# Loading q's weight matrix with five DMAs of 128 rows instead of one

## The chip, the cores and the metric

The kernel runs on one core of one Trainium2 chip. The time is the device time of one execution in microseconds; the median of the runs counts. A profile is one more execution, taken with the hardware profiler; its span runs from the first instruction to the last, and the execution's own time has some 1.8 us around it.

## The reference

A transformer block in the parallel form: one layer norm feeds an attention and a feed-forward network, and both results are added to the input. The attention is local and dilated: each position looks at 8 positions, 0, 2, ..., 14 steps back, with 32 heads of 20 numbers each. S is 2048, D is 640, F is 1536, all in bf16.

```
xn  = layernorm(x)                                     # (S, D)
q, k, v = split(xn @ wqkv)                             # wqkv: (640, 1920), 32 heads of 20
logits[h, s, w] = q[h, s] . k[h, s - 2 w] * 20**-0.5   # w = 0..7, masked where s - 2 w < 0
attn = softmax(logits, over w)
o[h, s] = sum_w attn[h, s, w] * v[h, s - 2 w]
out = x + o @ wo + gelu(xn @ w1 + b1) @ w2 + b2        # w1: (640, 1536), w2: (1536, 640)
```

## The kernel before

The 2048 positions are handled in four chunks of 512, each of four blocks of 128 rows. A block is normalised with its rows on the partitions (`xn`), then transposed so that the 640 features lie on the partitions in five slices of 128 (`xnT`). For chunk 0 the transposes are done by TensorE (`do_tp`, L280) and copied out of PSUM by VectorE or ScalarE (`do_tc`, L285); for the other chunks a DMA transposes. q, k and v of a chunk are 15 groups of matmuls over the five slices; attention products and sums are done by VectorE; the feed-forward network's first layer goes through L586 and both output projections are summed in PSUM by L622 and L624.

The order of all work on all engines is written out by hand: the table ORDER names every piece once, and each engine runs its instructions in that order. Nothing is rescheduled; a wait on an engine holds all that stands behind it there.

The change lies ahead of this table, in the loads that are issued at the kernel's start. Most are issued by SP, one after the other, and share 16 DMA engines with the two that ScalarE issues. In order, SP's are: block 0 of x (`load_x(0, 1)`, L130), q's weights, k's weights (`load_w`, L133), blocks 2 and 3 of x, v's weights, blocks 4 to 7, and w1 in two halves (L146). Blocks 8 to 15 follow where `ldx` stands in ORDER. ScalarE issues block 1 (L137) and the 12 rows of the bias b1 (L138). The weights of q, k and v are columns 0 to 639, 640 to 1279 and 1280 to 1919 of the matrix in memory; each lands in a tile of 128 partitions x 5 x 640 (`wq_sb`, `wk_sb`, `wv_sb`), where the second index, written t in the view `wqkv_v`, is the group of 128 rows, that is, the slice of `xnT` that it is multiplied with.

Each DMA counts up one of eight semaphores as it lands, and the DMAs of SP and ScalarE take these eight in turn; a DMA that takes a semaphore again waits for the earlier one on it.

On TensorE the start runs like this. Ones are multiplied until block 0 is there (`do_warm`, L446). Block 0 is transposed in two parts, slices 0 and 1 (`tp00a`) and slices 2 to 4 (`tp00b`); the bias is transposed (`tb`, L456). Then q of block 0 is computed slice by slice: for each slice ti five matmuls of 128 columns, one for each output tile (`q_piece`, L349; the pieces are `ga` for slices 0 and 1, `gb2`, `gb3`, `gb4`). The transpose of block 1 (`tp01`) stands between `gb2` and `gb3`; q of block 1 follows (`gd` and `ge`, 25 matmuls), then k of blocks 0 and 1 (`hj100` to `hj102`, L380, 25 matmuls of 256 columns), the transpose of block 2 (`tp02`), five matmuls of v, the transpose of block 3 (`tp03`), and so on. Statistics of blocks 0, 2 and 3 are taken by VectorE (L209, L211), the square root by ScalarE (L245), reciprocal and normalisation by VectorE (L251, L265).

The order around the change, from the table's first lines:

```
wa ho st00a sum1 st00 rs00 rc00 neg1 sq1 xn00a tp00a wb xn00b tp00b mean1 tc00a rs01 rc01 tb b1 tc00b ga gb2 xn01 tp01
tc01a tc01b gb3 gb4 gd ge gc4 gc1 hj100 st02a st02 rs02 hc100 st03a st03 hj101 gc0 rc02 xn02 rs03 hj102 rc03 xn03
hc101 hc102 tp02 tc02 hj202 tp03 tc03 hj201 ...
```

Of the kernel before, what the change touches and what calls it, by code (L numbers as in the profile page):

```python
# [16 lines left out]
S, D, F, H, W, DIL = 2048, 640, 1536, 32, 8, 2  # L17
# [3 lines left out]
KT, FT = D // P, F // P  # L21
# [54 lines left out]
def kernel(  # L76
# [16 lines left out]
    nc = tc.nc  # L93
# [24 lines left out]
    wqkv = [wts.tile([P, KT, D], BF16, name=f"w{s}_sb") for s in "qkv"]  # L118
# [6 lines left out]
    wqkv_v = A_wqkv.rearrange("(t p) n -> p t n", p=P)  # L125
# [6 lines left out]
    def load_w(s):  # L132
        nc.sync.dma_start(wqkv[s][:], wqkv_v[:, :, s * D : (s + 1) * D])  # L133
# [2 lines left out]
    nc.vector.memset(x_sb[:, 1, 0:16], 0.0)  # L136
    nc.scalar.dma_start(x_sb[:, 1, :], x_nb[:, 1, :])  # L137
    nc.scalar.dma_start(b1_rt[0:FT, :], B_b1.rearrange("(t p) -> t p", p=P))  # L138
    load_w(0)
    load_w(1)  # L140
    load_x(2, BPC)
    load_w(2)
# [645 lines left out]
```

## Time and profile before

| what | value |
|---|---|
| median of 3 runs | 207.1 us (206.86 to 207.37) |
| the profiled execution: time | 207.49 us |
| the profiled execution: span | 205.7 us |
| granted TensorE clock | 1.00 |
| busy: TensorE, VectorE, ScalarE, GpSimd | 98%, 85%, 62%, 17% of the span |
| q's weights: issue, KB, time to landing | 1.20 us, 800 KB, 5.5 us |
| read from HBM, written to it | 10.00 MB, 7.54 MB |

The loads of the start fill the 16 DMA engines until about 20 us; in this row of the profile each figure is the mean of one of 40 equal slices (5.14 us) of the span:

```profile
GB/s 210 390 397 370 75 232 326 403 102 185 64 116 264 99 186 181 142 192 124 207 198 113 144 107 64 0 16 182 41 0 132 162 193 162 192 41 17 30 52 64
```

Columns of a timeline line are the start in us, the duration, engine, line, operation and tiles, and in brackets the idle time before it and what ended that. PE is TensorE's matmul, PEld its weight load, DVE VectorE, ACT ScalarE, POOL GpSimd, SP SyncE; a q behind the name (SPq) is the engine's own instruction queue, from which it issues DMAs.

### The profile page before, as it was taken

The page shows a single profiled execution, that of the slowest core. Times are in us where ns is not written, and L with a number is a line of the kernel's source. Part 1 is how long each engine was busy: PE and PEld are TensorE (multiplying, and loading weights), DVE is VectorE, ACT ScalarE, POOL GpSimd, SP SyncE. Part 2 cuts the span into 40 slices and gives each one's busy share as a digit, 9 for nine tenths or more (in the row PEclk, how much of TensorE's full clock was granted, in tenths as well). Part 3 has the DMA queues.
Part 4 walks back from the last instruction along what each step waited for, and adds up shares of the span by engine and source line. Part 5 has one row for each costly group of instructions (what it writes and reads, how often), then busy time and mean ns, then how long its engine had stood idle before and what let it go on. Part 6 is the DMA issues. An engine that isn't in the chain of part 4 may idle for free.

```text
span 205.7 us, 3262 instructions
## 1 busy us (share of the span) xinstructions
PE 200.8 (98%) x1285; PEld 112.2 (55%) x1285; DVE 175.4 (85%) x214; ACT 127.7 (62%) x242; POOL 34.4 (17%) x49
## 2 busy tenths in 40 slices
PE   7899999999999999999999999999999999999994
PEld 2797745565445555555555554555444555555552
DVE  3489999379998989949999994999979979799981
ACT  5488999899999879916466344834616854221210
POOL 2000000050000422102703303001023420311210
DMA  6999389969258599899996965018209998931244
GB/s 210 390 397 370 75 232 326 403 102 185 64 116 264 99 186 181 142 192 124 207 198 113 144 107 64 0 16 182 41 0 132 162 193 162 192 41 17 30 52 64
DMA packets 27335, 31.77 MB, mean 154 GB/s; under 512 B 9272, under 2 KB 22072, under 8 KB 27320
## 3 DMA queue, kind: packets, MB, share of 16 engines
q0 software_dynamic: 7408, 12.78, 39.4%
q1 hardware_dynamic: 19600, 18.58, 31.4%
q8 instruction: 10, 0.16, 0.3%
q10 hardware_dynamic: 312, 0.20, 0.3%
q14 instruction: 5, 0.04, 0.1%
HBM read 10.00 MB, written 7.54 MB: 85 GB/s over the span
## 4 chain that ended last, share of the span: by engine, by line
PE 95%; DMA 3%; SPq 0%; DVE 0%; issue 0%
PE lo L622 29%; PE hps L586 25%; PE pps L336 24%; PE hi L624 7%; PE gps L380 7%; DMA wq_sb<-in_A_wqkv_dram 3%; PE L L474 2%; PE gps L349 1%; PE tp L280 0%; SPq L130 0%; DVE osb L652 0%
## 5 line engine op out<-in xcount | busy, mean ns | idle before, releaser
L586 PE MATMUL hps<-xnT,w_sb 128*128 128x512 bf16 x240 | 55.6, 379 | 0.0
L433 DVE TENSOR_TENSOR half<-qT,kT 128x2560 bf16<-128x2560 bf16 x32 | 46.2, 1482 | 2.9 <-PE L L474 2.8
L622 PE MATMUL lo<-w_sb,hT 128*128 128x512 bf16 x144 | 41.3, 379 | 0.0
L586 PEld LDWEIGHTS <-w_sb 128*128 128x128 bf16 x240 | 22.9, 98 | 26.3 <-issue 0.8
L629 ACT CAST osb<-lo 128x512 bf16<-128x512 f32 x15 | 8.8, 587 | 36.8 <-PE hi L624 18.5
L624 PE MATMUL hi<-w_sb,hT 128*128 128x128 bf16 x144 | 31.5, 219 | 0.0
L602 ACT ACTIVATE hT<-hps,b1T 128x512 bf16<-128x512 f32 x36 | 24.0, 683 | 10.7 <-PE hps L586 10.7
L465 DVE TENSOR_TENSOR half<-half 128x2048 bf16<-128x2048 bf16 (+1 forms) x32 | 29.0, 952 | 0.2
L635 POOL DMA_DIRECT2D out_dram<-osb x15 | 13.6, 973 | 77.1 <-ACT osb L630 68.5
L557 DVE TENSOR_TENSOR half<-vT,x_sb 128x2560 bf16<-128x2560 bf16 x16 | 22.8, 1485 | 4.4 <-DMA x_sb<-e 3.0
L557 DVE TENSOR_TENSOR half<-vT,ax 128x2560 bf16<-128x2560 bf16 x16 | 22.8, 1485 | 2.3 <-PE L L474 1.4
L622 PEld LDWEIGHTS <-hT 128*128 128x128 bf16 x144 | 14.1, 98 | 16.8
L622 PE MATMUL lo<-wo,oT 128*128 128x512 bf16 x80 | 23.1, 379 | 0.0
L567 POOL DMA_DIRECT2D half<-half x12 | 14.3, 1195 | 48.9 <-DVE half L557 48.5
L336 PE MATMUL pps<-xnT,wv_sb 128*128 128x512 bf16 x75 | 18.5, 379 | 0.0
L336 PE MATMUL pps<-xnT,wq_sb 128*128 128x512 bf16 x75 | 18.3, 379 | 0.0
L336 PE MATMUL pps<-xnT,wk_sb 128*128 128x512 bf16 x75 | 17.7, 379 | 0.0
L624 PE MATMUL hi<-wo,oT 128*128 128x128 bf16 x80 | 16.9, 219 | 0.0
L173 ACT ACT_TABLE_LOAD x12 | 15.4, 1283 | 0.9 <-PEq L772 0.7
L624 PEld LDWEIGHTS <-hT 128*128 128x128 bf16 x144 | 14.1, 98 | 2.2
L573 DVE TENSOR_TENSOR half<-half 128x1280 bf16<-128x1280 bf16 x16 | 13.1, 820 | 1.3 <-DMA half<-half 1.2
L622 PEld LDWEIGHTS <-oT 128*128 128x128 bf16 x80 | 7.8, 98 | 9.4
(91 smaller groups left out, 263.7 us busy)
## 6 DMA issues: line engine op xcount, KB each, us to landing
half<-half POOLq DMA_DIRECT2D x12, 640.0 KB, 7.1
w_sb<-in_B_w_dram SPq DMA_DIRECT2D x4, 960.0 KB, 11.0
out_dram<-osb POOLq DMA_DIRECT2D x15, 160.0 KB, 4.0
ax<-e SPq DMA_DIRECT2D x8, 256.0 KB, 4.8
x_sb<-e SPq DMA_DIRECT2D x8, 256.0 KB, 4.8
out_dram<-b2bc POOLq DMA_DIRECT2D x3, 640.0 KB, 8.7
x_sb<-in_A_x_dram SPq DMA_DIRECT2D x1, 1280.0 KB, 12.9
out_dram<-x_sb SPq DMA_DIRECT2D x2, 640.0 KB, 8.7
```

The source lines that it names most:

```text
L173: nc.scalar.activation(warm[:], nc.const_aps.tensor(0.0, [P, 1], F32), func)
L336: nc.tensor.matmul(ps[:], lhsT=wqkv_p[which][:, ti, to, :], rhs=xnT[:, ti, :], start=(ti == 0), stop=(ti == KT - 1),)
L380: nc.tensor.matmul(ps[:, to - a, :], lhsT=wqkv_p[which][:, ti, to, :], rhs=tiles["xnT", 0][:, ti, pair * 2 * P : (pair + 1) * 2 * P], star ...
L433: nc.vector.tensor_tensor(out=half[:, j, h], in0=q[:, :, at].unsqueeze(1).to_broadcast([P, W // 2, KT, P]), in1=window(k, h, at), op=ALU.mult,
L465: nc.vector.tensor_tensor(out=kept, in0=kept, in1=gone, op=ALU.add)
L557: nc.vector.tensor_tensor(out=half[:, j, h], in0=window(qkv_tile(n, 2), h, cs), in1=ax_view(n)[:, j, ws, :].unsqueeze(2).to_broadcast([P, ...
L567: nc.gpsimd.dma_start(a, b, accum_op=ALU.add, max_dma_last_dim=CUT)
L586: nc.tensor.matmul(ps[:], lhsT=w1_sb[:, ti, ft * P : (ft + 1) * P], rhs=tiles["xnT", n][:, ti, :], start=(ti == 0), stop=(ti == KT - 1),)
L602: nc.scalar.activation(hT, tiles["hps", n, ft][:], ACT.Gelu_apprx_tanh, bias=b1T[:, ft : ft + 1], scale=1.0)
L622: nc.tensor.matmul(lo[:], lhsT=lhs, rhs=rhs[:, 0:CH], start=first, stop=last)
L624: nc.tensor.matmul(hi[:, 0 : D - CH], lhsT=lhs, rhs=rhs[:, CH:D], start=first, stop=last)
L635: nc.gpsimd.dma_start(rows, tiles["osb", n, bl][:], accum_op=ALU.add)
```

## The change

The one DMA for q's weights is replaced by five, one for each group of 128 rows, into the same tile and from the same queue. Everything else, ORDER included, is as before. Each group of matmuls that uses a slice of the tile now waits for that slice's DMA. Four more of the eight semaphores are taken, so that a later load waits for another one of its predecessors than before. Behind the change all lines of the file are two lines further down.

```diff
     nc.vector.memset(x_sb[:, 1, 0:16], 0.0)
     nc.scalar.dma_start(x_sb[:, 1, :], x_nb[:, 1, :])
     nc.scalar.dma_start(b1_rt[0:FT, :], B_b1.rearrange("(t p) -> t p", p=P))
-    load_w(0)
+    for a in range(5):
+        ks = slice(a * KT // 5, (a + 1) * KT // 5)
+        nc.sync.dma_start(wqkv[0][:, ks, :], wqkv_v[:, ks, 0:D])
     load_w(1)
     load_x(2, BPC)
     load_w(2)
```

## The prediction

> **What bounds the kernel now.** I read the page first (busy time), then the chain of work that ended last, in order of time, then the waits of TensorE, then the timeline of the first 20 us, and last the DMA issues and a table of one-microsecond stages.
>
> ```profile
> PE 200.8 (98%) x1285; PEld 112.2 (55%) x1285; DVE 175.4 (85%) x214; ACT 127.7 (62%) x242; POOL 34.4 (17%) x49
> ```
>
> TensorE is busy for 200.8 of 205.7 us. The chain says where the other time is, and the waits of TensorE (line and releaser: us in total, times, longest) say it again:
>
> ```profile
> 1.20 5.51 DMA wq_sb<-in_A_wqkv_dram
> 6.76 1.03 PE gps L349 x15
> ```
>
> ```profile
> PE tp L280 <- DVE xn L265: 0.8, 1, 0.8
> ...
> PE gps L349 <- DMA wq_sb<-in_A_wqkv_dram: 0.6, 1, 0.6
> ```
>
> The chain hangs on the load of q's weights until 6.71 (1.20 + 5.51), and from 6.76 on it is TensorE almost to the end. TensorE has no recorded wait after that, so a microsecond won or lost there goes through to the end unless a later hand-over is tighter than it. The part of its idle time that this load causes is 0.6 us. That is all the change can win at its place.
>
> The timeline (start, duration, engine, line, operation) shows what else could have gone on then, and what comes 6 us later:
>
> ```profile
> 1.20 0.42 SPq L133 DMA_DIRECT2D wq_sb<-in_A_wqkv_dram  x1
> 1.67 0.52 SPq L133 DMA_DIRECT2D wk_sb<-in_A_wqkv_dram  x1
> 2.23 0.53 SPq L130 DMA_DIRECT2D x_sb<-in_A_x_dram  x1
> ...
> 5.76 0.29 DVE L285 COPY xnT<-tp 128x256 bf16<-128x256 bf16 x1
> 6.00 0.18 PE L456 MATMUL tb<-ident,b_rt 16*128 16x16 bf16 x1
> ...
> 9.60 0.89 DVE L209 BATCH_NORM_STATS2 stats<-x_sb 128x6 f32<-128x320 bf16 x2 [1.20 <-DMA x_sb<-in_A_x_dram]
> ...
> 11.79 0.45 DVE L265 TENSOR_SCALAR xn<-x_sb,mv,rstd 128x640 bf16<-128x640 bf16 x1
> 12.48 0.38 PEld L280 LDWEIGHTS <-xn 128*128 128x128 bf16 x5
> ```
>
> The first two slices of xnT, which the first ten matmuls on q need, are there at 6.05 (5.76 + 0.29). VectorE sat idle before 9.60 until blocks 2 and 3 of x landed; the normalised block 2 that follows from them is ready at 12.24 (11.79 + 0.45), and TensorE takes it at 12.48. So this hand-over has 0.24 us to spare, and 0.06 of that is the usual step between the engines (an earlier one: xn ends at 5.66, TensorE starts at 5.72).
>
> ```profile
> wk_sb<-in_A_wqkv_dram SPq DMA_DIRECT2D x1, 800.0 KB, 7.1
> ...
> x_sb<-in_A_x_dram SPq DMA_DIRECT2D x1, 320.0 KB, 7.3
> ```
>
> ```profile
> 2.00:3.00 1.00, 1.00 (x4) 0.43 (x3) 0.00 (x0) 0.22 (x2) 0.00 (x0) 1.00 0.88 269
> 3.00:4.00 1.00, 1.00 (x5) 0.36 (x4) 0.72 (x2) 0.37 (x1) 0.00 (x0) 1.00 1.02 328
> 4.00:5.00 1.00, 0.65 (x6) 0.32 (x4) 0.54 (x3) 0.93 (x5) 0.00 (x0) 1.00 1.04 386
> ```
>
> The last column is SDMA GB/s, the one before it the share of the 16 engines: from 2 us on they are full (0.88, 1.02, 1.04), up to 20 us. The loads are one stream; each lands when the bytes ahead of it are through. wk lands at 1.67 + 7.1 = 8.8, blocks 2 and 3 at 2.23 + 7.3 = 9.5.
>
> **Part 1: the first matmuls on q start earlier.** They need the first piece instead of all five. Bytes through, by the stage rows: 0.04 MB before 2.0, then 0.269, 0.328 and 0.386 a microsecond, 1.02 MB by 5.0. Block 0, block 1 and all of q are 1120 KB = 1.15 MB, through at 5.3; q landed 1.4 us later, at 6.7. By the same count the pieces are through at 3.5, 4.0, 4.4, 4.8 and 5.3, and with the same 1.4 us land at about 4.9, 5.4, 5.8, 6.2 and 6.7. TensorE is done with tb at about 6.1 and wants the pieces at 6.1, 6.5, 6.8, 7.4 and 7.8 (five matmuls take 0.35 us: 1.03 / 15 x 5; five transposes stand between the third and the fourth). All are there. Gain at this place: 6.76 - 6.1 = 0.6 us, and 50 matmuls on q end near 9.4 instead of 10.0. Then wk is wanted at 9.2 (its weight load started at 9.80) and has landed at 8.8: no wait.
>
> **Part 2: what takes the gain back.** The 25 matmuls on wk (2.73 us) then end some 0.6 us earlier, and the next thing on TensorE is the transpose of block 2. It can't start before 12.24 + 0.06 = 12.30, since its chain hangs on the landing at 9.5, not on TensorE: statistics of both blocks, square root, reciprocal, L265. So TensorE arrives 0.6 early and waits 0.4: of the 0.6 us, 12.48 - 12.30 = 0.18 stays. Block 3's hand-over is like it (L265 ends at 13.10, TensorE takes it at 13.30). Behind them the half of w1 that landed at about 18.5 is taken at 19.03, with 0.4 to spare, more than 0.18. I found no later hand-over from VectorE that is tighter: the sums for the logits end at 36.13 and are taken at 36.53.
>
> **Part 3: what the four added DMAs cost.** SP issues one in 0.42 us, with 0.46 to 0.47 from issue to issue (0.74, 1.20, 1.67). wk's issue moves from 1.67 to 1.20 + 5 x 0.46 = 3.50, and all of SP's loads behind it move. Data begins to move at 1.8 (the DMA view of the first two microseconds), 1.06 us after the first issue, so wk could move from 4.56; its turn is at 5.3. That is 0.7 us of cover, by which the added issues cost nothing; the work that hides them is the stream itself, already queued. If an issue takes what the next two took (0.52, 0.53, so 0.57 from one to the next), wk can move from 5.1 and the cover is 0.2; by the small bias load on ScalarE's queue (0.64) it is 0.36 late. Bounds of this cost: 0 to 0.36; I take 0, since 0.42 is the row of the same tensor.
>
> Also, eight completion semaphores are used in turn, so from the ninth load on each waits for an earlier one. In the changed program wk waits for block 0 (landed at 0.74 + 2.5 = 3.2, before SP gets there), blocks 2 and 3 for q's first piece, wv for its second, blocks 4 to 7 for block 1, the halves of w1 for q's third piece and the bias, blocks 8 to 15 for q's fourth. Before, the first two of these waits stood at the halves of w1. Blocks 2 and 3 are then issued at about 4.9 and can move from 6.0; their turn is at 5.3 + 2.1 = 7.4. wv is issued at about 5.4, can move from 6.5, and its turn is at 8.2. Behind the waiting load stand all later loads of SP, and each has over a microsecond of cover. Cost 0; without cover, each microsecond late goes to TensorE but for the 0.18.
>
> The price of a border between two transfers in the stream has no row of its own. From above: block 0 alone, 160 KB, took 2.5 us to land, 2.1 more than its bytes at 390 GB/s. From below: blocks 2 and 3 land 0.7 us after wk, for 320 KB, which at 390 GB/s are 0.84; nothing is left for the border. I take 0, as the queue is full there just as it will be for q. A gain is possible too: in 1.8 to 3.8 us the stream ran at 174, 287, 315 and 329 GB/s in half-microsecond stages, 0.58 us behind a steady 390; pieces that read the matrix in another order may lose less or more there.
>
> **Sum.** -0.6 at q, +0.4 at block 2's transpose, 0 for issues, waits and borders: -0.2 us. The profiled execution took 207.5 (span 205.7 and 1.8 around it), 0.4 above the median of 207.1; so 207.3 for a like execution, and 206.9 for the median.
>
> **Rivals.**
> 1. The landing of blocks 2 and 3 comes earlier with the pieces. Place: the stream before 4 us. For it: the 0.58 us lost there. Against it: q's bytes and rows are the same. From 0.4 us earlier on, nothing takes the gain back: -0.6, so 206.5.
> 2. The stream falls behind (the other side). Place: SP's queue. Its price is the time by which a load is ready after its turn, and it decides from 0.2 us on, when block 2's transpose comes later than now. For it: wk's cover falls from 2.6 us (1.67 + 1.06 against 5.3) to 0.7, and a piece (0.42 us of data at 390 GB/s) takes 0.46 to issue. Against it: the cover above. If none of it holds, the whole shift of wk's issue shows, 1.8 us: blocks 2 and 3 at 11.3, TensorE 1.6 late, 208.7; with half, 207.8.
> 3. The change doesn't do what it says: the pieces land together, near 6.7, as completions come late on a full queue. For it: q landed 1.4 us after its bytes were through. Then 207.1.
> 4. Every transfer carries its lone overhead in series: four times 2.1 us. Blocks 2 and 3 at 17.9, TensorE 8.2 late, 215.3. Against it: the 0.7 us between wk and blocks 2 and 3.
>
> Beside rival 4 stands a rule of the Trainium skill, "DMA: Bandwidth & Descriptors", sections "Anatomy of one DMA" and "Rules for kernel authors": it fits about 2.0 us fixed per DMA on GpSimd's path, and asks for transfers of 1 MiB and more, small ones being joined. By that fit in series four more transfers would be an estimated 8 us. The trace doesn't agree where the queue is full, by the 0.7 us for 320 KB.
>
> **How the numbers follow.** Forecast 0.50, rival 1 0.17, rival 2 0.23, rival 3 0.07, rival 4 0.03. A measurement of this kernel tells about 0.3%, 0.62 us, from no change; the three runs shown lie 0.5 us apart. Faster by more: half and a little of rival 1 (its 0.6 sits at the bound), 0.10, and 0.02 of the forecast's scatter: 0.12. Slower by more: most of rival 2, 0.19, rival 4, 0.03, and 0.02 of scatter: 0.24. Within: 0.64. The range takes in rival 1 and the part of rival 2 up to some 0.8 us: 206.4 to 207.9, leaving out about 0.18. The likeliest case alone: 206.6 to 207.2.
>
> **What would show it.** Right: the first L349 at about 6.1, no DMA wait of q among TensorE's waits, in its place a wait of the transpose (L280) for L265 of about 0.4 us near 12; blocks 2 and 3 landing at 9.5; wk issued near 3.5. Part 1 is wrong if L349 still waits for a piece; part 3 is wrong if the stage rows before 8 us fall below 380 GB/s or blocks 2 and 3 land after 9.7. The forecast falls if that landing moves by more than 0.4 us either way, or if a later hand-over shows a new wait of TensorE.

## The result, and the profile after

The changed kernel takes 210.47 us (median of 6 runs, 209.93 to 212.05), the kernel before 207.26 us (6 runs, 206.86 to 207.44): slower by 3.2 us, a ratio of 1.0165 with a 95% interval of 1.0131 to 1.0198. The forecast was 206.9 us, its range 206.4 to 207.9. The profiled execution took 210.40 us, its span is 208.6 us, 2.9 more than before.

First the timeline of the changed kernel, for the same places as in the prediction (start, duration, engine, line, operation; in brackets the idle time before and what ended it). All lines are two further down, so L349 is L351, L280 is L282, L209 is L211 and L265 is L267:

```profile
1.21 2.31 SPq L141 DMA_DIRECT2D wq_sb<-in_A_wqkv_dram  x5
3.56 0.44 SPq L133 DMA_DIRECT2D wk_sb<-in_A_wqkv_dram  x1
4.05 0.52 SPq L130 DMA_DIRECT2D x_sb<-in_A_x_dram  x1
...
6.04 0.75 PE L351 MATMUL gps<-xnT,wq_sb 128*128 128x128 bf16 x10
...
11.65 0.89 DVE L211 BATCH_NORM_STATS2 stats<-x_sb 128x6 f32<-128x320 bf16 x2 [3.97 <-DMA x_sb<-in_A_x_dram]
...
13.84 0.45 DVE L267 TENSOR_SCALAR xn<-x_sb,mv,rstd 128x640 bf16<-128x640 bf16 x1
14.34 0.45 PE L282 MATMUL tp<-ident,xn 128*128 128x128 bf16 x5 [0.58 <-DVE xn L267]
```

The first matmuls on q start at 6.04 instead of 6.76, as forecast. But the statistics of blocks 2 and 3, which started at 9.60, now wait for their DMA until 11.65, and the transpose of block 2 starts at 14.34 instead of 12.48 (there its weight load, which the prediction shows; its matmul stood at 12.59): some 1.8 us late. The DMA view (KB, us from issue to landing) and the waits of TensorE say what else came late:

```profile
wq_sb<-in_A_wqkv_dram SPq DMA_DIRECT2D x5, 160.0 KB, 3.6
wk_sb<-in_A_wqkv_dram SPq DMA_DIRECT2D x1, 800.0 KB, 7.2
...
x_sb<-in_A_x_dram SPq DMA_DIRECT2D x1, 320.0 KB, 7.6
```

```profile
PE gps L382 <- DMA wk_sb<-in_A_wqkv_dram: 1.5, 1, 1.5
PE tp L282 <- DVE xn L267: 1.2, 2, 0.6
```

wk lands at 3.56 + 7.2 = 10.8 instead of 8.8, blocks 2 and 3 at 4.05 + 7.6 = 11.6 instead of 9.5. TensorE waits 1.5 us for wk and the rest in front of block 2. The issues are not at fault: wk's stands at 3.56 for a forecast of 3.50, blocks 2 and 3 are issued at 4.05 for about 4.9, and SP was held by no semaphore before either. The stream itself lost the time. Stage rows (last column GB/s, before it the share of the DMA engines):

```profile
3.00:4.00 1.00, 1.00 (x5) 0.32 (x4) 0.79 (x2) 0.42 (x1) 0.00 (x0) 1.00 0.99 340
4.00:5.00 1.00, 0.77 (x7) 0.36 (x5) 0.50 (x4) 0.94 (x5) 0.00 (x0) 1.00 0.72 133
5.00:6.00 1.00, 0.63 (x8) 0.47 (x8) 0.96 (x4) 0.97 (x3) 0.00 (x0) 1.00 0.93 324
...
8.00:9.00 1.00, 1.00 (x22) 1.00 (x20) 0.00 (x0) 0.20 (x1) 0.00 (x0) 1.00 1.01 311
```

From 4 to 5 us, where it had 386 GB/s, it has 133, and until 10 us it stays between 303 and 348 where it had 374 to 396. In the stall eight packets take 420 to 850 ns each, for 55 ns elsewhere.

The 16 DMA engines don't come through together, and a load has landed when the last of them has. Blocks 2 and 3 were through on eight engines by 8.56 before and by 9.55 after, on 15 by 8.92 and by 10.85, on the last by 9.58 and by 11.63, with the statistics starting at 9.60 and 11.65. So about 1.0 us of the 2.05 is common to the engines, and the rest lies in the slowest of them.

The shift of TensorE, matmul against matmul, stays at 1.76 to 1.83 us up to 180 us and is 2.06 at the last matmul (0.2 come at 183 us, where ScalarE waits for an output buffer until an output DMA has landed). The span is 2.9 us longer. So 0.8 us are lost behind the last matmul. The end of the kernel before and then of the changed one, in the timeline (a line of several matmuls ends at start plus duration):

```profile
core 0 of [0], span 205.7 us
...
202.51 0.44 PE L624 MATMUL hi<-wo,oT 128*128 128x128 bf16 x5
202.82 0.36 SPq L644 DMA_DIRECT2D out_dram<-osb  x1
...
203.31 0.37 ACTq L657 DMA_DIRECT2D out_dram<-osb  x1
```

```profile
core 0 of [0], span 208.6 us
...
204.57 0.44 PE L626 MATMUL hi<-wo,oT 128*128 128x128 bf16 x5
204.87 0.36 SPq L646 DMA_DIRECT2D out_dram<-osb  x1
...
205.37 0.37 ACTq L659 DMA_DIRECT2D out_dram<-osb  x1
```

From the last matmul's end to the end of the span it is 2.78 us before (202.95 to 205.73) and 3.60 after (205.01 to 208.61). The last two output DMAs are issued with the same distance to the matmul, and land with it: 1.61 and 1.8 us behind it in both. What follows them differs. SP waits for the eight DMA semaphores, 103 to 110, one after the other. The trace's records of these waits, by their start in us behind the last matmul's end:

```
before: last DMAs on 109 and 110. waits: 103 0.60, 104 0.67, 105 0.74, 106 0.80, 107 0.86, 108 0.92, 109 1.63, 110 1.88, drain 1.95
after:  last DMAs on 105 and 106. waits: 103 0.49, 104 0.55, 105 1.63, 106 1.89, 107 1.95, 108 2.01, 109 2.07, 110 2.16, drain 2.64
```

With four more DMAs the turn has moved on by four, so that the last two landings stand third and fourth in SP's list. Of the 0.82 us that the end is longer, 0.28 are the rest of the list (110 is through at 2.16 for 1.88), 0.41 are a longer step from there to the drain (0.48 for 0.07), and 0.13 come behind the start of the drain.

### The profile page after: what moved, and what is told of

Read it like the earlier page. It is cut to its first block, busy times and chain, and to the rows that moved or that the text cites. A ratio compares the mean times of both kernels' runs of the same rounds, so it can differ in the third digit from the quotient of the medians.

```text
span 208.6 us, 3244 instructions
## 1 busy us (share of the span) xinstructions
PE 200.3 (96%) x1263; PEld 112.2 (54%) x1285; DVE 175.4 (84%) x214; ACT 127.6 (61%) x242; POOL 34.4 (17%) x49
## 4 chain that ended last, share of the span: by engine, by line
PE 87%; DMA 6%; SPq 1%; DVE 1%; issue 1%; ACT 1%; ACTq 0%
PE lo L624 25%; PE hps L588 25%; PE pps L338 23%; PE hi L626 7%; PE gps L382 5%; DMA x_sb<-in_A_x_dram 4%; DMA out_dram<-osb 3%; PE L L476 2%; SPq L141 1%; DVE stats L211 1%; ACT osb L631 1%; PE tp L282 0%; DVE xn L267 0%; SPq L133 0%; DVE mv L213 0%
## 5 line engine op out<-in xcount | busy, mean ns | idle before, releaser
L588 PE MATMUL hps<-xnT,w_sb 128*128 128x512 bf16 x229 | 55.0, 379 | 0.6
L624 PE MATMUL lo<-w_sb,hT 128*128 128x512 bf16 x139 | 40.3, 379 | 0.1
## 6 DMA issues: line engine op xcount, KB each, us to landing
x_sb<-in_A_x_dram SPq DMA_DIRECT2D x1, 1280.0 KB, 12.4
```

Of the source, the lines that this page charges most:

```text
L588: nc.tensor.matmul(ps[:], lhsT=w1_sb[:, ti, ft * P : (ft + 1) * P], rhs=tiles["xnT", n][:, ti, :], start=(ti == 0), stop=(ti == KT - 1),)
L624: nc.tensor.matmul(lo[:], lhsT=lhs, rhs=rhs[:, 0:CH], start=first, stop=last)
```

## The experiments

The theories, in the order in which they came up. A: the loads have less lead over their turn. B: small DMAs are slow as such. C: the first reading of the matrix's later rows stalls, later put as C' (whoever reads unread rows piece by piece meets a slow start each time). D: small pieces at the start of the stream. L: a cut DMA stalls where its turn comes some 2 us after its issue; S, N and P are its rivals. R: the semaphore list at the end. M: the place of the tiles in memory. All times are medians; "before" is measured beside each group (207.2 to 207.3 us). Edits are against the kernel before, unless the changed one is named.

**Less lead alone.** q in one DMA; the loads behind it are held by a write into wk's tile until 3.52 us, close to where wk's issue stands in the changed kernel.

```diff
-    load_w(1)
 ...
+        nc.gpsimd.memset(wqkv[1][:, 0:3, :], 0.0)
+        load_w(1)
```

> q's weights are loaded by one DMA as before; only the issue of k's weights, and with it all SP loads behind it, is held back by a GpSimd fill of the tile until about 3.5 us (1.67 before, 3.56 in the changed kernel). Theory A (lead: the loads behind q are issued too late, so that engines come to the end of their queue and lose a microsecond each time): blocks 2 and 3 land at 11 to 12 us instead of 9.6, TensorE's transpose of block 2 some 2 us later, 209 to 210.5 us in all. Theory B (pieces: the borders of small transfers, or reading the matrix by row groups, slow the stream): they land at 9.6 to 9.8 and the time is 207.1 to 207.5.

207.46 us, ratio 1.0018 (1.0005 to 1.0031). The stage rows show one dip where wk's turn comes and then the full stream:

```profile
5.00:6.00 1.00, 0.53 (x7) 0.40 (x7) 0.94 (x5) 0.97 (x3) 0.00 (x0) 1.00 1.00 312
6.00:7.00 1.00, 1.00 (x18) 0.95 (x17) 0.73 (x4) 0.62 (x2) 0.00 (x0) 1.00 1.06 384
```

A falls as the whole cause: late issues of whole DMAs cost 0.2 us here by the median. (The profiled run, 208.67 us, is the slowest of the ten: there one DMA engine was late on blocks 4 to 7, which were through on 15 engines by 12.85 and on the last by 14.51. Blocks 2 and 3 landed at 9.16.)

**Small DMAs deep in the stream.** v by three DMAs.

```diff
-    load_w(2)
+    for ks in (slice(0, 2), slice(2, 4), slice(4, 5)):
+        nc.sync.dma_start(wqkv[2][:, ks, :], wqkv_v[:, ks, 2 * D : 3 * D])
```

> q by one DMA as before; v's weights, which are issued some 5 us before their turn, by three DMAs of 256, 256 and 128 rows. Theory A (lead): nothing is lost, blocks 4 to 7 land at 13.2 to 13.6 us, the stage rows from 8 to 11 us stay at 390 GB/s, 207.0 to 207.6 us. Theory B (pieces): the stage rows from 8 to 11 us fall below 360 GB/s and blocks 4 to 7 land 0.5 to 1.5 us later than 13.35.

207.68 us, ratio 1.0028 (1.0015 to 1.0042). In the stages of v's transfer nothing is lost:

```profile
8.00:9.00 1.00, 1.00 (x22) 1.00 (x20) 0.00 (x0) 0.20 (x1) 0.00 (x0) 1.00 1.07 393
9.00:10.00 1.00, 1.00 (x14) 1.00 (x12) 0.64 (x2) 0.65 (x2) 0.00 (x0) 1.00 1.08 396
```

B falls. (The 0.4 us belong to the end: 3.26 us behind the last matmul.)

**q in two DMAs, and q's five in another order.** In the changed kernel the loop becomes, in the one run, two DMAs of 2 and 3 row groups, and in the other five in the order 2, 0, 1, 3, 4.

```diff
-    for a in range(5):
-        ks = slice(a * KT // 5, (a + 1) * KT // 5)
+    for ks in (slice(0, 2), slice(2, 5)):
```

> q's weights by two DMAs, rows 0 to 255 and 256 to 639; one more issue on SP, so k's weights are issued at about 2.15 us instead of 1.67 or 3.56. Theory A (lead): most of the lead is kept, blocks 2 and 3 land at 9.5 to 10.0, the first matmul on q at 6.05, 206.9 to 207.5 us. Theory B (a loss for every border, 2.05 us over four): 0.5 us later per border, blocks 2 and 3 at 10.1, 207.4 us; the stall at 4 to 5 us is there in part.

> The five DMAs of the changed kernel in another order: rows 256 to 383 first, then 0, 128, 384, 512. Theory A (lead): the stall stands at the same time, 4 to 5 us, whichever rows are read there, and blocks 2 and 3 land at 11 to 12 us; 209.9 to 211 us. Theory C (the first read of rows from 256 on meets something slow in memory, which one DMA over all rows overlaps): the slow stretch moves to the first piece, about 3 us, and 4 to 5 us runs at over 300 GB/s.

208.76 us (1.0056 to 1.0105) and 209.64 us (1.0072 to 1.0149). The stage 4 to 5 us of the one and of the other:

```profile
4.00:5.00 1.00, 1.00 (x4) 0.29 (x3) 0.50 (x4) 0.97 (x5) 0.00 (x0) 1.00 0.77 233
```

```profile
4.00:5.00 1.00, 0.62 (x6) 0.32 (x4) 0.50 (x4) 0.95 (x5) 0.00 (x0) 1.00 0.71 161
```

One cut is enough, and the stall stays at its time whichever rows are read first: C falls as it was put. Both times lie above what I had expected under every theory. The trace of the one cut is of its slowest run (209.68 us); its blocks 2 and 3 landed at 11.4, nearly as late as behind four cuts (11.6).

**Rows read once before, and pieces of an unread matrix.** In the changed kernel a small DMA ahead of q's five reads a few bytes of every row, or of every sixteenth; in the kernel before, w1's first half is cut in five.

```diff
+    touch = consts.tile([P, KT, 8], BF16, name="touch")
+    nc.sync.dma_start(touch[:], wqkv_v[:, :, 0:8])
```

```diff
+    touch = consts.tile([8, KT, 8], BF16, name="touch")
+    nc.sync.dma_start(touch[:], A_wqkv.rearrange("(t p s) n -> p t s n", p=8, s=16)[:, :, 0, 0:8])
```

```diff
-        nc.sync.dma_start(w1_sb[:, :, cs], w1_v[:, :, cs])
+    for ks in [slice(a, a + 1) for a in range(5)]:
+        nc.sync.dma_start(w1_sb[:, ks, 0 : F // 2], w1_v[:, ks, 0 : F // 2])
+    nc.sync.dma_start(w1_sb[:, :, F // 2 :], w1_v[:, :, F // 2 :])
```

> The changed kernel with one DMA more: ahead of q's five pieces, a DMA reads 16 bytes of each of the 640 rows of the weight matrix into a spare tile that nothing reads. Theory C' (the pieces are slow because q is the first to read these rows, and one piece after another meets rows that nobody has read, which the single DMA meets all at once): with the rows read once before, the stall of the five pieces is gone; the stage 4 to 5 us is above 330 GB/s instead of 133, and x blocks 2-3 land, counted from their issue, within 6.3 us instead of 7.6; the small DMA itself costs up to some 1 us of the stream, so 207.3 to 208.7 us. Theory D (small pieces at the start of the stream are slow whatever was read before): a stage of under 240 GB/s stays between 4 and 6 us, x blocks 2-3 land at 11.5 us or later, 209.5 to 211.5 us.

> As the kernel with the small DMA over all rows, but the small DMA reads 16 bytes of every sixteenth row only (40 rows). C' with a coarse unit (16 rows, some 60 KB, or more): no stall in the stage 4 to 5 us and 207.0 to 208.0 us, less than with all rows. C' with a fine unit (single rows): the stall stays and the time is 209.5 to 210.7 us. D: the same as the fine unit.

> The kernel before, q whole, with the first half of w1 by five DMAs of 128 rows (nobody has read these rows; they stand deep in the stream, behind x blocks 4-7). C': the pieces meet unread rows one after another, so a stage between 12 and 17 us falls under 300 GB/s, and w1's second half lands 1 us or more later than in the kernel before. D: stages stay at 390 GB/s or above through 16 us. Under both the time stays within 0.4% of before, 206.8 to 208.0 us, since w1 is needed only long after.

211.69 us (1.0177 to 1.0223), 211.03 us (1.0167 to 1.0219) and 208.15 us (1.0033 to 1.0067). The second kernel's stages show the stall a microsecond earlier, and the third's, in w1's transfer, show none:

```profile
3.00:4.00 1.00, 1.00 (x4) 0.31 (x3) 0.81 (x2) 0.41 (x1) 0.00 (x0) 1.00 0.76 146
4.00:5.00 1.00, 1.00 (x7) 0.46 (x5) 0.50 (x4) 0.97 (x5) 0.00 (x0) 1.00 0.81 232
```

```profile
12.00:13.00 1.00, 0.76 (x10) 0.70 (x10) 0.85 (x3) 1.00 (x5) 0.00 (x0) 1.00 1.07 398
13.00:14.00 1.00, 1.00 (x14) 0.99 (x13) 0.69 (x2) 0.95 (x2) 0.00 (x0) 1.00 1.09 399
```

C' falls on both sides: reading the rows before doesn't help, and unread rows in pieces leave the stream's rate alone when they stand deep in it. They weren't free, though. The first piece was through on 15 engines by 13.34 and on the last by 15.48, w1's second half landed at 19.59 (18.60 in the kernel before), and TensorE, 0.27 us ahead until then, waited for it:

```profile
PE hps L586 <- DMA w_sb<-in_B_w_dram: 0.6, 1, 0.6
```

It was 0.5 us late from there on, and 3.59 us stand behind its last matmul. The trace is of a run of 208.81 us, above the median. Nor is the stall bound to a time. The two kernels with the small DMA were slower than I had expected under either theory; one cause is in the last group below.

**Blocks 2 and 3 ahead of wk.** A test of the explanation, and the version most likely to beat both.

```diff
-    load_w(1)
-    load_x(2, BPC)
+    load_x(2, BPC)
+    load_w(1)
```

> The kernel before, q whole, with the DMA of x blocks 2-3 issued ahead of wk's. The explanation of the changed kernel's time (transpose of block 2 is pinned by the landing of x blocks 2-3, and what follows it keeps that shift to the end): x blocks 2-3 land 1.5 to 2.1 us earlier, at 7.5 to 8.0, block 2's transposes start up to 1.5 us earlier unless another wait takes over; wk lands 0.8 us later, at 9.5, where TensorE turns to wk within its 0.7 us of cover, so 0 to 0.5 us is lost there; 205.6 to 207.2 us. Rival (the landing of x blocks 2-3 is not what sets the later work; wk's landing is): 207.4 to 208.3 us.

207.16 us, ratio 1.0004 (0.9995 to 1.0014): no gain. Blocks 2 and 3 land at 1.67 + 5.2 = 6.9, and the normalised block 2 is ready at 11.42, but TensorE comes to it only at 12.11, from its own work. So in the kernel before their landing is not what sets the pace; it does so from about 9.5 on, which is where it stood.

**Five pieces with much lead, and the same with little.** wk is cut instead of q: in its place (issued from 1.67, turn at 5.2), and held back as in the first experiment (issued from 3.52, turn at 5.3).

```diff
-    load_w(1)
+    for a in range(5):
+        nc.sync.dma_start(wqkv[1][:, a : a + 1, :], wqkv_v[:, a : a + 1, D : 2 * D])
```

```diff
+        nc.gpsimd.memset(wqkv[1][:, 0:3, :], 0.0)
+        for a in range(5):
+            nc.sync.dma_start(wqkv[1][:, a : a + 1, :], wqkv_v[:, a : a + 1, D : 2 * D])
```

> The kernel before, q whole, with wk by five DMAs of 128 rows in wk's place: the first is issued at 1.67 us and its transfer is due at some 5.2 us, behind q, so the pieces have 3.5 us between issue and transfer, where q's pieces in the changed kernel had 1.8. Theory L (a piece whose transfer is due some 2 us after its issue is slow, one with more lead is not) and theory S (only the DMAs that follow in the first 2 us of the stream are slow): stages 5 to 9 us stay at 370 GB/s or above, x blocks 2-3 land by 9.7, 206.9 to 207.9 us. Theory N (five small DMAs slow the stream wherever they stand among the first weights): a stage under 300 GB/s between 5 and 8 us, x blocks 2-3 land after 10.5, 208.3 us or more.

> The kernel in which wk's issue was held by a GpSimd memset until 3.5 us (207.46 us with wk whole), now with wk by five DMAs of 128 rows: the pieces are issued from 3.5 to 5.4 us and each transfer is due some 2 us behind its issue, as q's pieces in the changed kernel, but 2 us later in the stream. Theory L: a stage under 280 GB/s between 5 and 8 us, x blocks 2-3 land 1 us or more behind the 9.7 that the issue times alone give, at 10.7 or later, 208.5 us or more. Theory S: stages from 6 us on at 345 GB/s or above, x blocks 2-3 land by 10.3, 207.2 to 208.2 us.

208.43 us (1.0044 to 1.0083) and 211.00 us (1.0134 to 1.0227). The same five DMAs of the same bytes, first with 3.5 us between issue and turn, then with 1.8:

```profile
6.00:7.00 1.00, 1.00 (x18) 0.90 (x16) 0.84 (x4) 0.60 (x2) 0.00 (x0) 1.00 1.07 389
7.00:8.00 1.00, 1.00 (x22) 1.00 (x20) 0.29 (x1) 0.13 (x1) 0.00 (x0) 1.00 1.06 370
```

```profile
6.00:7.00 1.00, 1.00 (x15) 0.78 (x13) 0.73 (x4) 0.55 (x2) 0.00 (x0) 1.00 0.93 192
7.00:8.00 1.00, 1.00 (x22) 1.00 (x20) 0.29 (x2) 0.00 (x0) 0.00 (x0) 1.00 0.75 209
```

This is L, and neither S nor N. The first of the two has no stall in wk's transfer and yet lies 0.5 us above my range: it has 3.59 us at its end. Its stages 8 to 10 us are at 335 and 338, where the load of blocks 2 and 3 has its turn; a semaphore had held its issue until 5.78, so it too had little lead, but in the profiled run (207.98 us) the last matmul ends at 202.60, as early as in any kernel here with q whole, so this dip cost nothing there. What the median's other 0.45 us are, no trace shows.

**q by halves of the partitions.**

```diff
-    for a in range(5):
-        ks = slice(a * KT // 5, (a + 1) * KT // 5)
-        nc.sync.dma_start(wqkv[0][:, ks, :], wqkv_v[:, ks, 0:D])
+    for h in (slice(0, 64), slice(64, 128)):
+        nc.sync.dma_start(wqkv[0][h, :, :], wqkv_v[h, :, 0:D])
```

> The kernel before with q by two DMAs of 64 partitions each (all five row groups in each), issued at 1.21 and 1.67 us. q by two DMAs cut between row groups gave 208.76 us, with 233 GB/s in the stage 4 to 5 us. If the number and the lead of the DMAs matter (L and S): the stage 4 to 5 us is under 280 GB/s and 208.2 to 209.5 us. If the addresses matter (all engines reading within one or two groups of 128 rows): no stall, 206.9 to 207.7 us.

212.19 us (1.0224 to 1.0285). This tells nothing on the addresses, since it brings costs of its own: packets take 94 ns in place of 55 from 5.5 to 8 us, as the second half passes (55 while the first does), the stages 6 to 8 us have 223 GB/s, and the granted clock is 0.50 from 10 to 13 us, after TensorE has waited 2.1 us for q.

**One cut of q, with two leads.** In the changed kernel q goes by two DMAs of 4 and 1 row groups, or of 1 and 4; the second is issued at 1.67 in both, and its turn is at some 4.7 or at 3.5.

```diff
-    for a in range(5):
-        ks = slice(a * KT // 5, (a + 1) * KT // 5)
+    for ks in (slice(0, 4), slice(4, 5)):
```

> q by two DMAs, 4 row groups and then 1: the second is issued at 1.67 us and due at some 4.7, a lead of 3.0 us, where the cut 2 and 3 gave 2.3 us and 233 GB/s in the stage 4 to 5 us. Theory L (the stall comes where a DMA's transfer is due some 2 us behind its issue): no stage from 4 to 8 us under 330 GB/s, x blocks 2-3 land by 10.3; with the 0.7 us that one added DMA costs at the end, 207.6 to 208.2 us. Theory N (any cut of q stalls the stream where the border passes): a stage under 260 GB/s between 4 and 6 us, 208.5 to 209.3 us.

> q by two DMAs, 1 row group and then 4: the second is issued at 1.67 us and due at 3.5, a lead of 1.8 us. Theory L: stall at or above that of the cut 2 and 3, a stage under 240 GB/s between 3 and 5 us, x blocks 2-3 land at 11 us or later, 208.6 to 210 us. Theory P (the stall grows with the number of small DMAs in a row, not with the lead): a stall no deeper than that of the cut 2 and 3 (233 GB/s), 207.7 to 208.8 us.

208.44 us (1.0038 to 1.0074) and 210.09 us (1.0109 to 1.0164). Stages of the cut 4 and 1, then of 1 and 4:

```profile
4.00:5.00 1.00, 1.00 (x7) 0.46 (x5) 0.50 (x4) 0.92 (x5) 0.00 (x0) 1.00 1.06 386
5.00:6.00 1.00, 0.78 (x11) 0.48 (x8) 0.92 (x4) 0.97 (x3) 0.00 (x0) 1.00 1.03 334
```

```profile
4.00:5.00 1.00, 1.00 (x6) 0.44 (x5) 0.53 (x3) 0.97 (x5) 0.00 (x0) 1.00 0.64 155
...
9.00:10.00 1.00, 1.00 (x12) 1.00 (x11) 0.01 (x1) 0.00 (x0) 0.00 (x0) 0.50 1.06 385
```

With about 3 us of lead there is no stall and blocks 2 and 3 land at 9.1; with 1.8 the stream drops to 227, 155 and 251 GB/s from 3 to 6 us and they land at 11.0. L and not N or P. The time of the cut 1 and 4 holds more than the stall: TensorE waited 1.8 us for q, and then the granted clock was 0.50 to 0.55 from 8 to 11 us (0.50 in the second line shown), by which its lateness grows from 1.15 to 2.7 us. The clock fell in two of its four runs (210.90 and 210.63 us); the other two took 209.56 us, and that is the price without it. The median is 0.09 us above my range. The cut 4 and 1 lies 0.24 us above its range. Its TensorE was 0.75 us ahead until 16 us and lost that waiting for w1, whose halves landed at 16.78 and 19.15, the last engine 1.5 us behind the 15th. It ends 0.06 us behind the profile of before, which is 0.3 to 0.4 behind a run whose q isn't late, and 3.46 us stand behind its last matmul.

**The end alone.** Four DMAs of 128 x 16 bytes are added at some 35 us, to the kernel before and to the changed one, first into a tile among the constants, then into one behind all others; and that first tile is added without any DMA.

```diff
         nc.sync.dma_start(b2bc[:], b2_bcast)
+        for a in range(4):
+            nc.sync.dma_start(spare[:, a, :], x_nb[:, 0, 8 * a : 8 * a + 8])
```

> The kernel before, q whole, with four small DMAs more (128 x 16 bytes each, of x into a spare tile that nothing reads), issued by SyncE some 35 us after the start, behind b2bc's load: nothing is changed in the first 30 us. Theory R (the end waits for eight DMA semaphores in a fixed order; they go round with each DMA of SyncE and ScalarE, so four more DMAs put the two last output DMAs on the third and fourth semaphore of that list instead of the last two, and SyncE has to work off the rest of the list after the last landing): from the last matmul's end to the end of the span 3.60 us instead of 2.78, 207.8 to 208.2 us. Rival (the longer end of the changed kernel comes from its late start or from a disturbed output DMA): 2.78 us, and 207.0 to 207.4 us.

> The changed kernel with the same four small DMAs at some 35 us: eight added DMAs in all, so the two last output DMAs are back on the last two semaphores. R: 2.78 us from the last matmul's end to the end of the span instead of 3.60, so 209.4 to 209.9 us where the changed kernel took 210.47. Rival: 3.6 us or more, 210.2 to 210.9 us.

> The kernel before with a tile of 64 bytes in each partition allocated ahead of x and the weights (one element of it is written at the start, nothing reads it), so that all of them lie 64 bytes further on, at 20544 instead of 20480 and so on; no DMA is added. In the four kernels with such a tile the stream ran at 357 to 376 GB/s from 6 to 14 us where the others have 390 to 400. Theory M (the place of the tiles, 64 bytes off a multiple of 128, slows the stream): stages from 6 to 14 us at 355 to 378 GB/s, TensorE waits 0.4 to 1 us for w1 near 18 us, the end is 2.78 us behind the last matmul, 207.8 to 208.6 us. Rival (the small DMAs slowed the stream): 390 GB/s or above, 207.0 to 207.4 us.

> The kernel before with the four late small DMAs, into a tile allocated behind all others, so that x and the weights lie where they lay. R: stages as in the kernel before (390 GB/s or above), 3.60 us from the last matmul's end to the end of the span, 207.8 to 208.2 us. Rival: 207.0 to 207.4 us.

> The changed kernel with the four late small DMAs into a tile behind all others: what is left of the change when its cost at the end is taken out and the tiles lie where they lay. R: 2.78 us from the last matmul's end, x blocks 2-3 land at 11.3 to 12, 209.4 to 209.9 us. Rival: 3.6 us, 210.2 to 210.9 us.

| run | time, us | ratio, 95% interval | last matmul to end, us |
|---|---|---|---|
| before + four, tile among the constants | 209.18 | 1.0071 to 1.0104 | 3.60 |
| changed + four, tile among the constants | 209.96 | 1.0116 to 1.0155 | 2.79 |
| before + tile alone | 208.21 | 1.0034 to 1.0058 | 2.80 |
| before + four, tile behind all | 208.08 | 1.0028 to 1.0062 | 3.58 |
| changed + four, tile behind all | 209.08 | 1.0059 to 1.0101 | 2.80 |

The last column is within 0.02 us of what R had put on record, 3.60 and 2.78. Four DMAs that change nothing else, the fourth row, cost 0.87 us; in the changed kernel four more, eight in all, take the 0.8 us off again. The end of the fourth run and of the fifth in their timelines:

```profile
core 0 of [0], span 206.3 us
...
202.33 0.39 PE L628 MATMUL hi<-wo,oT 128*128 128x128 bf16 x4
```

```profile
204.21 0.44 PE L630 MATMUL hi<-wo,oT 128*128 128x128 bf16 x5
204.52 0.36 SPq L650 DMA_DIRECT2D out_dram<-osb  x1
```

Over all runs the length of the end goes with the place of the two last landings among 103 to 110, whatever else was changed: 2.8 us on 109 and 110, 3.26 on 103 and 104, 3.5 on 110 and 103 or on 106 and 107, 3.6 on 105 and 106.

R's reason, the rest of the list, covers only 0.3 of the 0.8 us. Most of the rest is a stop of 0.4 to 0.5 us in SP's list, and its place moves too, one instruction towards the front for each DMA added. With one more it stands ahead of the drain (2.63 to 3.12 us behind the last matmul), with four between the wait for 110 and the drain (2.16 to 2.64), with five between the waits for 109 and 110 (2.02 to 2.50), and with eight between those for 106 and 107 (0.95 to 1.43 in the second row's run), ahead of the last landings, where it costs nothing. Place of the landings and number of DMAs go together in all these runs, so they don't tell whether one follows from the other, and that eight is the number of semaphores isn't shown to be why the stop does no harm there.

The fifth run lies 0.3 us under my range. Its stream came back sooner (370, 362 and 361 GB/s from 6 to 9 us, against 343, 348 and 311), but blocks 2 and 3 landed at 11.53 all the same, 0.1 sooner than in the changed kernel; as far as the traces tell, the rest is the 0.2 us at 183 us, which this run doesn't have. Its six runs lie between 208.06 and 209.47 us.

The third row is M: the tile of 64 bytes alone, which moves x and the weights by 64 bytes, costs 1.0 us. A stage of that run:

```profile
8.00:9.00 1.00, 1.00 (x22) 1.00 (x20) 0.24 (x1) 0.48 (x1) 0.00 (x0) 1.00 1.07 366
```

In the kernel before the same stage has 396 at the same share of the engines:

```profile
8.00:9.00 1.00, 1.00 (x22) 1.00 (x20) 0.29 (x1) 0.48 (x1) 0.00 (x0) 1.00 1.07 396
```

TensorE then takes at 20.02, after a wait for w1, the half of w1 that it took at 19.03. The first two rows carry this cost besides the end (0.9 and 1.0 us make up the first row's 1.9, which was far over my range), and so do the two kernels with the small read ahead of q.

No version beat the kernel before.

## Why the prediction was wrong

*Part 1 was right of the profile, and worth less than it seemed.* The first L351 is at 6.04 for a forecast of 6.1, and no piece of q is waited for. But the 0.6 us that this part could win is that one execution's. Its q landed on 15 of the 16 DMA engines by 5.76 and on the last at 6.71. In nine other kernels that load q whole ahead of all pieces, q landed between 5.8 and 6.2, and where the tiles lay as before TensorE took it between 6.04 and 6.48. Their last matmul ended at 202.6 to 202.7 us where nothing else came late, against 202.95 in that profile. So there was next to nothing to win in a usual run.

*Part 2 had the hand-over right.* Block 2's transpose follows the landing of blocks 2 and 3. Where q was early and that landing stayed (w1 in five, 9.59), the transpose came at 12.30, the forecast's figure, with 0.18 gained. In the changed kernel the landing moved by 2.05 us and the transpose by about 1.8. What bounds a gain next is w1's half, which TensorE took at 19.03: it landed at 18.6 to 18.8 in kernels with a usual q, so some 0.3 us can go on to the end (their last matmul ended at 202.6 to 202.7).

*Part 3 is the step that failed,* and within it the term "The price of a border between two transfers", taken as 0 "as the queue is full there just as it will be for q". What was full was the stream as the kernel before feeds it: wk's turn came 3.6 us after its issue. The cover of 0.7 us was counted from the first data 1.06 us after the first issue, and the issues did come in time by that count. The step from the last byte to the landing was mis-sized as well: of the 1.4 us that the prediction added, 0.5 held on 15 engines and 0.95 were the one late engine, so the first two pieces landed at 3.97 and 4.58 for forecasts of 4.9 and 5.4. That one did no harm. The runs show that the count of the cover isn't enough: cut DMAs with 1.8 to 2.3 us between issue and turn stall (133, 155, 192, 233 GB/s), those with 3 us or more don't (386, 389). The prediction's own sign of this, stage rows under 380 GB/s before 8 us and blocks 2 and 3 after 9.7, is what came, though the first half of it was badly put: the kernel before has 374 itself at 5 to 6 us, and only the 133 tells. The loss doesn't count borders either: one cut with little lead brought that landing to 11.4, four to 11.6. The prediction's upper bound, 2.1 us a border, wasn't passed, but that is luck: it prices each border, and the loss is one stall.

*Missing from the sum:* the end. Part 3 followed the semaphores' turn through the loads, where it cost nothing, and not to the end of the kernel, where it costs 0.82 us. The sum as it should have stood, against executions whose q isn't late: 2.3 to 2.4 us at the last matmul (205.01 against 202.6 to 202.7) and 0.8 behind it, 3.1 to 3.2; measured 3.21 between the medians.

*The rivals.* Rival 2 named the right side, place and hand-over, but its price was the shift of the issues, which the first experiment shows to cost 0.2 us in whole DMAs. That its full case came near (blocks 2 and 3 at 11.3, measured 11.6) is luck, and its 208.7 lacked the end. Rival 1 and rival 3 fell: the landing came later, and q's pieces landed one after another, 3.97 to 6.71. Rival 4 fell: four borders didn't cost 8 us. The Trainium skill's rule beside it, to join small transfers into large ones ("DMA: Bandwidth & Descriptors", section "Rules for kernel authors"), pointed the right way. By the fixed 2.0 us of its section "Anatomy of one DMA" in series it would have been an estimated 8 us, for 3.2 measured, and pieces that stood deep in the stream cost its rate nothing (393 to 399 GB/s).

*What stays open.* What happens in the stall isn't in the trace: packets take long, and nothing else is seen to move. Little lead alone doesn't make it, since the whole wk with 1.7 us of lead dipped only to 312 GB/s for one stage. Nor does smallness: the second DMA of the cut 1 and 4 has 640 KB, and with 1.8 us of lead the stream fell to 155. And of the 0.8 us at the end the list itself explains some 0.3; the stop of 0.4 to 0.5, whose place moves with the number of DMAs, is recorded but has no cause there.

## What to carry to other kernels

A load that is cut in pieces needs each piece issued well ahead of its turn (here 3 us and more was safe, about 2 was not); at the very start of a kernel there is no such lead, so cut later loads rather than the first, if any: no version with a cut beat the kernel before. Look at what stands behind the last landing: 1, 2, 4 or 5 added DMAs lengthened the end by 0.5 to 0.8 us wherever they stood, and 8 didn't. And before pricing a wait of half a microsecond at the start, see in a second profile whether it is there at all.

## What the hardware showed besides

- 64 bytes of displacement of the destination tiles slowed the stream of 1280-byte rows from 396 to 366 GB/s at the same busy share. The Trainium skill, "DMA: Bandwidth & Descriptors", section "How a descriptor splits into AXI transactions", counts an extra transaction for a descriptor that doesn't start at a multiple of 256 bytes. It says so of reads, and here it is the written side that moved (x from byte 20480 of each partition, a multiple of 256, to 20544); the run agrees in direction, with 7% less.
- A DMA over 64 of the 128 partitions took 94 ns a packet in place of 55 while the second of two such halves passed, and 55 while the first did.
- After a pause of TensorE of 1.8 to 2.1 us at 6 to 8 us, the granted clock was 0.50 for some 3 us; but it stayed at 1.00 after 1.4 us at 7 to 8.5 us (q in two), 1.5 to 1.65 us at 9 to 11 us, and 2.4 us at 12.4 to 14.8 us (wk in five with little lead). So the length of the pause alone doesn't decide it.
